# Attention with transposed AV in column tiles, packed exps and softmax sums gathered and broadcast by DMA

## Chip, cores, metric

One core of one Trainium2 chip. The time is the device time of one execution in microseconds (us). Executions of one kernel differ here, so each is listed with its mean granted TensorE clock (1.0 is full speed).

## The reference

Two independent parts, whose results are joined along the last axis. Part B (a state-space convolution, "the SSM") is the same in both kernels and runs first. Part A is attention over four segments of 512 rows, 32 heads of 18 numbers, with a memory carried from segment to segment:

```python
q, k, v = x @ wq, x @ wk, x @ wv              # 2048 x 576 -> 32 heads x 4 segments x 512 x 18
g = sigmoid(beta)                             # one gate per head
for s in range(4):
    p = softmax(q_s @ k_s.T * 18**-0.5 + causal_mask)
    a_dot = p @ v_s
    a_mem = (phi(q_s) @ M) / (phi(q_s) @ z + 1e-6)    # phi(t) = t + 1 if t > 0 else exp(t)
    o_s = g * a_mem + (1 - g) * a_dot
    M, z = M + phi(k_s).T @ v_s, z + phi(k_s).sum()
return concat(o) @ wo
```

## The kernel before

Four heads form a head group; each head has its own 32 rows of the array (18 used). Key block `kt` (128 keys) is scored against the queries from `128*kt` on, so a head's four blocks have 512, 384, 256 and 128 columns. V has a 19th column of ones, which makes the softmax sums. The product of the exps with V, called AV below, has the queries on partitions; so dividing by the sums is a product along the row, but the output must be transposed again before it meets `wo`.

```python
def scores_exp(s, hg, T, PT):
    for kt in range(4):
        for pr in range(2):                       # two heads to a score buffer
            pss = ps_s.tile([P, 2, L], F32, tag="s")
            for u in range(2):
                h4 = 2 * pr + u
                rows = slice(32 * h4, 32 * h4 + DH)
                nc.tensor.matmul(pss[:, u, P * kt:L], lhsT=T.kT[rows, hg, P * kt:P * kt + P],
                                 rhs=T.qT[rows, hg, P * kt:L], ..., tile_position=(32 * h4, 0))
            nc.scalar.activation(out=PT[kt][:, 2 * pr:2 * pr + 2, :], in_=pss[:, :, P * kt:L], func=ACT.Exp, ...)
        # [cut: causal mask of the diagonal block on GpSimd]

def av_retrieve(s, hg, T, PT, Oall, NDall, Mz_bd):
    po = ps_o.tile([P, 4, 4, DH + 1], F32, tag="o")
    for qt in range(4):
        for h4 in range(4):
            for kt in range(qt + 1):              # 40 matmuls of 19 columns
                nc.tensor.matmul(po[:, qt, h4, :], lhsT=PT[kt][:, h4, P * (qt - kt):P * (qt - kt) + P],
                                 rhs=T.Vaug[:, kt, 4 * hg + h4, :], ...)
    nc.vector.tensor_copy(out=Oall[:, :, 4 * hg:4 * hg + 4, :], in_=po[:])
    # [cut: retrieval from the memory, 4 matmuls of 76 columns, copied by ACT]

for s in range(NSEG):
    for hg in range(8):
        # [cut: allocation of PT]
        scores_exp(s, hg, T, PT)
        proj_chunk(s + 1, hg, Tn)                 # q, k, v, phi(k) of the next segment; none in segment 3
        av_retrieve(s, hg, T, PT, Oall, NDall, Mz_bd)
    # [cut: reciprocals and gates for the whole segment on DVE and GpSimd]
    for qt in range(4):                           # 5 transposes, their copies, 10 matmuls of 288 columns
        ...
```

The softmax here doesn't subtract the row's maximum and nothing guards it: scores larger than these inputs give would overflow.

Of the kernel before, what the change touches and what calls it, by code (L numbers as in the profile page):

```python
# [9 lines left out]
ALU = mybir.AluOpType  # L10
ACT = mybir.ActivationFunctionType
F32 = dt.float32
# [6 lines left out]
H = 32  # L19
# [16 lines left out]
def part_b(ctx, tc, B_q, B_k, B_v, B_shift_k, B_ssm_k, B_ssm_D, out, GB=288, debug=None):  # L36
# [25 lines left out]
    if debug == 'consts':  # L62
        nc.sync.dma_start(out=ov[:, 0, :], in_=CS[:, 0:9, :].rearrange('p a b -> p (a b)'))
        nc.sync.dma_start(out=ov[:, 1, :], in_=SN[:, 0:9, :].rearrange('p a b -> p (a b)'))
        nc.sync.dma_start(out=ov[:, 2, :], in_=CST[:, 0:9, :].rearrange('p a b -> p (a b)'))
        nc.sync.dma_start(out=ov[:, 3, :], in_=SNT[:, 0:9, :].rearrange('p a b -> p (a b)'))
        nc.sync.dma_start(out=ov[:, 4, 0:256], in_=W1bd[:].rearrange('p a b -> p (a b)'))
        nc.sync.dma_start(out=ov[:, 4, 256:320], in_=Psibd[:].rearrange('p a b -> p (a b)'))
        nc.sync.dma_start(out=ov[:, 4, 320:448], in_=ident[:])
        nc.sync.dma_start(out=ov[:, 5, :], in_=NSN[:, 8:17, :].rearrange('p a b -> p (a b)'))  # L70
        return
# [248 lines left out]
def part_a(ctx, tc, A_x, A_wq, A_wk, A_wv, A_wo, A_beta, out):  # L320
    nc = tc.nc
    consts = ctx.enter_context(tc.tile_pool(name="a_consts", bufs=1))
    segp = ctx.enter_context(tc.tile_pool(name="a_seg", bufs=2))
    accp = ctx.enter_context(tc.tile_pool(name="a_acc", bufs=1))
    hgp = ctx.enter_context(tc.tile_pool(name="a_hg", bufs=2))
    smallp = ctx.enter_context(tc.tile_pool(name="a_small", bufs=2))
    ps_s = ctx.enter_context(tc.tile_pool(name="a_ps_s", bufs=2, space=PSUM))
    ps_o = ctx.enter_context(tc.tile_pool(name="a_ps_o", bufs=1, space=PSUM))
    ps_j = ctx.enter_context(tc.tile_pool(name="a_ps_j", bufs=2, space=PSUM))

    scale = 1.0 / math.sqrt(DH)

    def load_w(w_ap, tail_at_64, nm):
        wt = consts.tile([P, 5, WPAD], BF16, tag=nm, name=nm)
        nc.vector.memset(wt[:, :, D:WPAD], 0.0)
        nc.sync.dma_start(out=wt[:, 0:4, 0:D], in_=w_ap[0:512, :].rearrange("(t p) f -> p t f", p=P))
        if tail_at_64:
            nc.sync.dma_start(out=wt[64:128, 4, 0:D], in_=w_ap[512:576, :])
        else:
            nc.sync.dma_start(out=wt[0:64, 4, 0:D], in_=w_ap[512:576, :])  # L340
        return wt

    wk_sb = load_w(A_wk, True, "wk_sb")
    wv_sb = load_w(A_wv, True, "wv_sb")
    wo_sb = load_w(A_wo, False, "wo_sb")

    def pad_w(w_sb, nm):
        wp = consts.tile([P, 5, H * 32], BF16, tag=nm, name=nm)
        nc.gpsimd.memset(wp[:], 0.0)
        nc.gpsimd.tensor_copy(out=wp[:, 0:4, :].rearrange("p t (h c) -> p t h c", c=32)[:, :, :, 0:DH],  # L350
                              in_=w_sb[:, 0:4, 0:D].rearrange("p t (h d) -> p t h d", d=DH))
        nc.gpsimd.tensor_copy(out=wp[64:128, 4, :].rearrange("p (h c) -> p h c", c=32)[:, :, 0:DH],
                              in_=w_sb[64:128, 4, 0:D].rearrange("p (h d) -> p h d", d=DH))
        return wp

    with tc.tile_pool(name="a_wtmp", bufs=1) as wtmp:
        wq_sb = wtmp.tile([P, 5, WPAD], BF16, tag="wq_sb", name="wq_sb")
        nc.sync.dma_start(out=wq_sb[:, 0:4, 0:D], in_=A_wq[0:512, :].rearrange("(t p) f -> p t f", p=P))
        nc.sync.dma_start(out=wq_sb[64:128, 4, 0:D], in_=A_wq[512:576, :])
        wq_pad = pad_w(wq_sb, "wq_pad")  # L360
    wk_pad = pad_w(wk_sb, "wk_pad")

    xT_all = consts.tile([P, 5, S], BF16)
    for t in range(5):
        c0 = 128 * t if t < 4 else 448
        nc.sync.dma_start_transpose(out=xT_all[:, t, :], in_=A_x[0, :, c0:c0 + P])

    def load_xT(s):
        return xT_all[:, :, L * s:L * (s + 1)]

    def kparts(t):
        return (slice(0, P) if t < 4 else slice(64, P))

    ident = consts.tile([P, P], BF16)
    nc.gpsimd.memset(ident[:], 0.0)
    nc.gpsimd.affine_select(out=ident[:], in_=ident[:], compare_op=ALU.not_equal, fill=1.0, base=0,
                            pattern=[[-1, P]], channel_multiplier=1)

    beta_bf = consts.tile([P, H], BF16)
    nc.sync.dma_start(out=beta_bf[:], in_=A_beta.partition_broadcast(P))  # L380
    g_bc = consts.tile([P, H], F32)
    nc.scalar.activation(out=g_bc[:], in_=beta_bf[:], func=ACT.Exp, scale=-1.0)
    nc.vector.tensor_scalar(out=g_bc[:], in0=g_bc[:], scalar1=1.0, scalar2=None, op0=ALU.add)
    nc.vector.reciprocal(out=g_bc[:], in_=g_bc[:])
    omg_bc = consts.tile([P, H], F32)
    nc.vector.tensor_scalar(out=omg_bc[:], in0=g_bc[:], scalar1=-1.0, scalar2=1.0, op0=ALU.mult, op1=ALU.add)

    Mz_f = consts.tile([P, 8, 19], F32)
    nc.vector.memset(Mz_f[:], 0.0)
    Mz_bds = [consts.tile([P, 8, 4 * (DH + 1)], BF16, tag="Mz_bd%d" % i, name="Mz_bd%d" % i) for i in range(2)]  # L390
    for i in range(2):
        nc.vector.memset(Mz_bds[i][:], 0.0)
    phikp = ctx.enter_context(tc.tile_pool(name="a_phik", bufs=1))

    def head_cols(w_pad, t, hg):
        return w_pad[kparts(t), t, 128 * hg:128 * hg + 128]

    o_view = out[0].rearrange("(j p) c -> p j c", p=P)

    class SegT:  # L400
        pass

    def alloc_seg(s):
        T = SegT()
        T.qT = segp.tile([P, 8, L], BF16, tag="qT")
        T.phiQ = segp.tile([P, 8, L], BF16, tag="phiQ")
        T.kT = segp.tile([P, 8, L], BF16, tag="kT")
        T.phiK = phikp.tile([P, 4, H * 32], BF16, tag="phiK")
        T.Vaug = segp.tile([P, 4, H, DH + 1], BF16, tag="Vaug")
        T.xT = load_xT(s)  # L410
        nc.gpsimd.memset(T.Vaug[:, :, :, DH:DH + 1], 1.0)
        if s < NSEG - 1:
            nc.gpsimd.memset(T.phiK[:], 0.0)
        return T

    def proj_chunk(s, hg, T):
        tok0 = 0
        xT = T.xT
        pq = ps_j.tile([P, L], F32, tag="pj")
        for t in range(5):  # L420
            nc.tensor.matmul(pq[:], lhsT=head_cols(wq_pad, t, hg), rhs=xT[kparts(t), t, tok0:tok0 + L],  # L421
                             start=(t == 0), stop=(t == 4))
        nc.vector.tensor_copy(out=T.qT[:, hg, :], in_=pq[:])  # L423
        if s > 0:
            e_sb = smallp.tile([P, L], BF16, tag="e_sb")
            nc.scalar.activation(out=e_sb[:], in_=pq[:], func=ACT.Exp)  # L426
            nc.vector.tensor_scalar(out=e_sb[:], in0=e_sb[:], scalar1=1.0, scalar2=None, op0=ALU.min)
            nc.vector.scalar_tensor_tensor(out=T.phiQ[:, hg, :], in0=pq[:], scalar=0.0, in1=e_sb[:],
                                           op0=ALU.max, op1=ALU.add)
        pk = ps_j.tile([P, L], F32, tag="pj")  # L430
        for t in range(5):
            nc.tensor.matmul(pk[:], lhsT=head_cols(wk_pad, t, hg), rhs=xT[kparts(t), t, tok0:tok0 + L],  # L432
                             start=(t == 0), stop=(t == 4))
        nc.scalar.copy(out=T.kT[:, hg, :], in_=pk[:])  # L434
        tt, half = hg // 2, hg % 2
        t0 = tok0 + P * tt
        c0 = 288 * half
        pv = ps_j.tile([P, 288], F32, tag="pj")
        for t in range(5):
            nc.tensor.matmul(pv[:], lhsT=xT[kparts(t), t, t0:t0 + P], rhs=wv_sb[kparts(t), t, c0:c0 + 288],  # L440
                             start=(t == 0), stop=(t == 4))
        nc.vector.tensor_copy(out=T.Vaug[:, tt, 16 * half:16 * half + 16, 0:DH],  # L442
                              in_=pv[:].rearrange("p (h d) -> p h d", d=DH))
        if s < NSEG - 1:
            pkt = ps_j.tile([P, 288], F32, tag="pj")
            for t in range(5):
                nc.tensor.matmul(pkt[:], lhsT=xT[kparts(t), t, t0:t0 + P], rhs=wk_sb[kparts(t), t, c0:c0 + 288],  # L447
                                 start=(t == 0), stop=(t == 4))
# [155 lines left out]
```

## Time and profile before

| | us | TensorE busy | ACT busy | DVE busy | mean clock |
|---|---|---|---|---|---|
| timed (three) | 620.52 median (619.65 to 628.27) | | | | |
| profiled execution | 637.5 | 82% | 48% | 47% | 0.728 |

A stage table of the profiled execution, from its windows. The columns are the window, its length, busy us (and instructions) of TensorE, its weight loads, DVE, ACT and GpSimd, then the clock, the DMA share and GB/s:

```profile
205.00:231.00 26.00, 5.54 (x13) 1.52 (x14) 1.92 (x8) 1.06 (x1) 18.97 (x11) 0.50 0.93 223
278.00:342.00 64.00, 58.80 (x561) 26.83 (x559) 30.80 (x62) 47.42 (x82) 20.91 (x31) 0.90 0.01 1
342.00:378.00 36.00, 36.00 (x265) 16.08 (x262) 13.49 (x51) 19.13 (x37) 9.12 (x10) 0.50 0.05 18
546.00:610.00 64.00, 52.40 (x509) 24.07 (x509) 11.08 (x28) 41.64 (x74) 24.39 (x32) 0.50 0.03 11
610.00:637.50 27.50, 15.91 (x60) 6.38 (x60) 9.85 (x21) 3.72 (x12) 0.00 (x0) 0.50 0.06 22
```

The start (205 to 231) is loading, with TensorE nearly idle. At a clock of 0.90 (second line) TensorE leaves 5 us of 64 idle; at half clock it is busy in all of 36 us (third). Segment 3 (fourth) and the last output product (fifth) are at half clock throughout.

### The profile page before, as it was taken

Reading aid. Unit: us, or ns where it says so; the run is one execution under the profiler, and the core shown is the slowest. Engines: PE = TensorE matmul, PEld = TensorE weight load, DVE = VectorE, ACT = ScalarE, POOL = GpSimd, SP = SyncE. Lnnn points to the kernel's source line nnn. Section 1 sums busy time; section 2 is a strip of 40 time slices with the busy share of each in tenths; the row PEclk is TensorE's granted clock in tenths of the full one; section 3 lists DMA queues with packets and bytes.
Section 4 is the critical chain, followed back from the end, with each engine's and each line's share of the span. In section 5 each row is a group of like instructions: output and inputs, shape, how many; then the busy total and the mean of one; then the engine's idle time right before and its main releaser. Section 6 shows DMA issues by size and latency. Waiting matters only on the chain.

```text
span 637.5 us, 9628 instructions
## 1 busy us (share of the span) xinstructions
PE 520.5 (82%) x3882; PEld 245.5 (39%) x3882; DVE 296.8 (47%) x611; ACT 302.9 (48%) x503; POOL 164.0 (26%) x189
## 2 busy tenths in 40 slices
PE   4186879799795179999997999999799999797646
PEld 1034547534474023434443443333344333343222
DVE  7994693734935023464444275332526433421041
ACT  2433523524233014437886545375645576647721
POOL 4000070000711900032333134121413222416310
PEclk9597999956998559959996558665556885555555
DMA  7978030040000930000000000000000000000000
GB/s 140 213 243 205 18 73 2 21 130 0 1 1 7 281 77 2 1 1 2 1 1 1 29 11 1 0 1 2 1 29 11 1 1 1 10 20 10 2 9 30
DMA packets 50431, 25.31 MB, mean 40 GB/s; under 512 B 32657, under 2 KB 49810, under 8 KB 50386
## 3 DMA queue, kind: packets, MB, share of 16 engines
q1 hardware_dynamic: 50386, 24.69, 15.9%
q8 instruction: 30, 0.49, 0.3%
q14 instruction: 15, 0.12, 0.1%
HBM read 9.75 MB, written 7.08 MB: 26 GB/s over the span
## 4 chain that ended last, share of the span: by engine, by line
PE 62%; DVE 16%; ACT 8%; issue 7%; POOL 3%; DMA 2%; SPq 2%; POOLq 0%; DVEq 0%; ACTq 0%
PE pss L464 10%; PE pout L556 7%; PE pk L432 6%; PE pq L421 6%; PE po L477 6%; ACT PT L466 5%; PE pv L440 5%; PE pkt L447 4%; DVE Y L269 2%; DVE A_sb L219 2%; PE ptr L545 2%; POOL PT L468 2%; DVE tmp L32 2%; PE pp L248 2%; PE ps L232 2%
## 5 line engine op out<-in xcount | busy, mean ns | idle before, releaser
L466 ACT ACTIVATE PT<-pss 128x1024 bf16<-128x1024 f32 (+3 forms) x256 | 171.9, 708 | 56.6 <-PE pss L464 55.1
L468 POOL TENSOR_SCALAR_AFFINE_SELECT PT<-PT 128x512 bf16<-128x512 bf16 x128 | 88.5, 695 | 260.6 <-ACT PT L466 250.1
L464 PE MATMUL pss<-qT,kT 18*128 18x256 bf16 (+3 forms) x512 | 99.6, 385 | 11.4 <-ACT PT L466 9.6
L421 PE MATMUL pq<-xT_all,wq_pad 128*128 128x512 bf16 (+1 forms) x160 | 59.0, 477 | 20.5 <-DMA xT_all<-in_A_x_dram 20.5
L477 PE MATMUL po<-Vaug,PT 128*128 128x19 bf16 x1280 | 52.6, 178 | 12.1 <-POOL PT L468 12.0
L276 POOL TENSOR_TENSOR Y<-xi_sb,H_sb 128x576 bf16<-128x576 bf16 x22 | 27.6, 1275 | 132.7 <-ACT xi_sb L275 132.2
L432 PE MATMUL pk<-xT_all,wk_pad 128*128 128x512 bf16 (+1 forms) x160 | 57.6, 453 | 1.4 <-DVE phiK L452 1.4
L477 PEld LDWEIGHTS <-PT 128*128 128x128 bf16 x1280 | 43.6, 103 | 33.6 <-POOL PT L468 23.2
L464 PEld LDWEIGHTS <-kT 18*128 18x128 bf16 x512 | 26.3, 96 | 63.0 <-issue 53.3
L556 PE MATMUL pout<-wo_sb,oT 128*128 128x288 bf16 (+1 forms) x160 | 46.9, 435 | 1.2 <-DVE oT L547 0.9
L423 DVE CAST qT<-pq 128x512 bf16<-128x512 f32 x32 | 22.1, 691 | 54.7 <-PE pq L421 30.5
L192 PE MATMUL ps<-kT,dg 128*128 128x512 bf16 x80 | 21.9, 438 | 23.4 <-DVE kvT L194 15.0
L440 PE MATMUL pv<-wv_sb,xT_all 128*128 128x288 bf16 (+1 forms) x160 | 34.0, 332 | 2.5 <-ACT kT L434 2.0
L479 DVE COPY Oall<-po 128x304 f32<-128x304 f32 x32 | 15.2, 474 | 43.3 <-PE po L477 43.0
L442 DVE CAST Vaug<-pv 128x288 bf16<-128x288 f32 x32 | 14.7, 460 | 43.3 <-PE pv L440 43.2
L421 PEld LDWEIGHTS <-wq_pad 128*128 128x128 bf16 (+1 forms) x160 | 14.6, 108 | 47.9 <-issue 26.1
L243 PE MATMUL pp<-A_sb,CS 128*128 128x288 bf16 x68 | 22.1, 326 | 13.1 <-ACT xi_sb L275 4.7
L232 PE MATMUL ps<-W1bd,xs 128*128 128x256 bf16 x144 | 23.2, 303 | 9.6 <-DMA xs<-in_B_ssm_k_dram 5.4
L547 DVE COPY oT<-ptr 128x128 bf16<-128x128 bf16 (+1 forms) x48 | 10.7, 222 | 40.0 <-PE ptr L545 40.0
L556 PEld LDWEIGHTS <-oT 128*128 128x128 bf16 (+1 forms) x160 | 17.8, 125 | 28.6 <-issue 21.4
L217 ACT CAST A_sb<-ps 128x1024 bf16<-128x1024 f32 x18 | 18.1, 1013 | 20.4 <-PE ps L232 20.1
L426 ACT ACTIVATE e_sb<-pq 128x512 bf16<-128x512 f32 x24 | 14.3, 596 | 28.1 <-DVE qT L423 28.1
(153 smaller groups left out, 787.3 us busy)
## 6 DMA issues: line engine op xcount, KB each, us to landing
q_sb<-in_B_q_dram SPq DMA_DIRECT2D x2, 1152.0 KB, 9.5
out_dram<-o_sb SPq DMA_DIRECT2D x2, 1152.0 KB, 7.2
out_dram<-outA SPq DMA_DIRECT2D x16, 144.0 KB, 1.7
kv_scratch<-kvT SPq DMA_DIRECT2D x4, 512.0 KB, 4.4
wq_sb<-in_A_wq_dram SPq DMA_DIRECT2D x1, 576.0 KB, 7.9
wk_sb<-in_A_wk_dram SPq DMA_DIRECT2D x1, 576.0 KB, 4.6
wv_sb<-in_A_wv_dram SPq DMA_DIRECT2D x1, 576.0 KB, 5.8
wo_sb<-in_A_wo_dram SPq DMA_DIRECT2D x1, 576.0 KB, 6.6
```

Of the source, the lines that this page charges most:

```text
L232: nc.tensor.matmul(ps[:, u, :], lhsT=xs[:, cc + u, :], rhs=W1bd[:].rearrange("p e k -> p (e k)"), start=True, stop=True)
L243: nc.tensor.matmul(pr, lhsT=CS[:, k1, :], rhs=A_sb[:, k1, :], start=True, stop=not (has_i or for_h))
L276: nc.gpsimd.tensor_tensor(out=Y4[:, k1, 2:4, :], in0=xi_sb[:].unsqueeze(1).to_broadcast([P, 2, GB]), in1=H_sb[:, k1, :, :], op=ALU.mult)
L421: nc.tensor.matmul(pq[:], lhsT=head_cols(wq_pad, t, hg), rhs=xT[kparts(t), t, tok0:tok0 + L], start=(t == 0), stop=(t == 4))
L432: nc.tensor.matmul(pk[:], lhsT=head_cols(wk_pad, t, hg), rhs=xT[kparts(t), t, tok0:tok0 + L], start=(t == 0), stop=(t == 4))
L440: nc.tensor.matmul(pv[:], lhsT=xT[kparts(t), t, t0:t0 + P], rhs=wv_sb[kparts(t), t, c0:c0 + 288], start=(t == 0), stop=(t == 4))
L447: nc.tensor.matmul(pkt[:], lhsT=xT[kparts(t), t, t0:t0 + P], rhs=wk_sb[kparts(t), t, c0:c0 + 288], start=(t == 0), stop=(t == 4))
L464: nc.tensor.matmul(pss[:, u, P * kt:L], lhsT=T.kT[rows, hg, P * kt:P * kt + P], rhs=T.qT[rows, hg, P * kt:L], start=True, stop=True, tile_ ...
L466: nc.scalar.activation(out=PT[kt][:, 2 * pr:2 * pr + 2, :], in_=pss[:, :, P * kt:L], func=ACT.Exp, scale=scale)
L468: nc.gpsimd.affine_select(out=PT[kt][:, :, 0:P], in_=PT[kt][:, :, 0:P], compare_op=ALU.is_ge, fill=0.0, base=0, pattern=[[0, 4], [1, P]], ...
L477: nc.tensor.matmul(po[:, qt, h4, :], lhsT=PT[kt][:, h4, P * (qt - kt):P * (qt - kt) + P], rhs=T.Vaug[:, kt, 4 * hg + h4, :], start=(kt == ...
L556: nc.tensor.matmul(pout[:], lhsT=oT[0:w, ft, :], rhs=wo_sb[0:w, ft, c0:c0 + 288], start=(ft == 0), stop=(ft == 4))
```

## The change

The intent: fewer and fuller instructions on the attention's path. The attention runs in sixteen slots, each for two head groups (a pair). A slot has ten exps of 1024 columns, which fill the score buffer, instead of sixteen of four widths; AV is turned round, so that V is the stationary operand, four heads work in four column tiles and the result has the head's numbers on partitions, ready for `wo` without a transpose. The softmax sums are then a row, one for each head, and dividing by them needs them on every partition of the head: they are gathered by small DMAs into a compact tile, inverted and gated, stored to DRAM and broadcast back. `wo` is laid out in eight padded groups. More changes with it: x is loaded by segment, the projections run two slots ahead and AV one slot behind, k is copied out by DVE instead of ACT, and four accumulation buffers serve projections, AV and output, where the kernel before had two for the projections and one each for AV and retrieval. Cut to its core:

```diff
-        for kt in range(4):
-            for pr in range(2):
-                ... nc.scalar.activation(out=PT[kt][...], in_=pss[:, :, P * kt:L], func=ACT.Exp)
+            for jj in range(2):                      # per head group: blocks 1 and 3 share a buffer
+                ps = self.ps_s.tile([P, 2, L], F32, tag="s", name="s1")
+                for b in range(2):
+                    mm(ps, b, 0, 2 * jj + b, u, 1)
+                for b in range(2):
+                    mm(ps, b, 384, 2 * jj + b, u, 3)
+                ex(p1[:, 2 * jj:2 * jj + 2, :], ps)
+        # block 2 of both head groups shares one (not shown)
-    nc.tensor.matmul(po[:, qt, h4, :], lhsT=PT[kt][:, h4, ...], rhs=T.Vaug[:, kt, 4 * hg + h4, :], ...)
+            for kt in range(4):
+                for j in range(4):
+                    nc.tensor.matmul(po[32 * j:32 * j + 32, P * kt:L], lhsT=V[:, kt, 19 * h:19 * h + 32], rhs=rhs,
+                                     start=(kt == 0), stop=(kt == 3), tile_position=(0, 32 * j))
+            nc.vector.tensor_copy(out=ou[:, u, 0, :], in_=po[:])
+        for j in range(4):                           # gather: 8 transfers
+            for u in range(2):
+                nc.sync.dma_start(out=cs[32 * j:32 * j + 16 * nk, u, :], in_=ou[32 * j + DH:..., u, :, :]...)
+        # [cut: reciprocal, times gate]
+        for j in range(4):                           # store: 8 transfers
+            for u in range(2):
+                nc.sync.dma_start(out=rd[j, u, 0:nk, :]..., in_=rb16[32 * j:32 * j + 16 * nk, u, :])
+        for j in range(4):                           # broadcast: 4 transfers
+            nc.sync.dma_start(out=rb[32 * j:32 * j + 32, :, :, :], in_=rd[j, :, 0:nk, :].partition_broadcast(32))
+        nc.vector.tensor_tensor(out=ou[:], in0=ou[:], in1=rb[:], op=ALU.mult)
-    nc.tensor.transpose(out=ptr[0:w, :], in_=o_seg[:, qt, P * ft:P * ft + w], identity=ident[:])   # and its copies
+    # beta is needed by partition: eight strided loads of 2-byte elements
+        for j in range(4):
+            nc.sync.dma_start(out=bt[32 * j:32 * j + 32, :], in_=gv[j].partition_broadcast(32))
+    def slot(self, i):
+        self.scores(s, p); self.proj_qk(i + 2); self.av(i - 1)
+        # then phi(k), memory update, v of the next segment, output product of the last one
```

## The prediction

> **What bounds the kernel now.** I read the span and the granted clock, then the page's slices, then the chain that ended last, then the groups by shape, then timelines of one head group. The page first:
>
> ```profile
> PE 520.5 (82%) x3882; PEld 245.5 (39%) x3882; DVE 296.8 (47%) x611; ACT 302.9 (48%) x503; POOL 164.0 (26%) x189
> PE   4186879799795179999997999999799999797646
> PEclk9597999956998559959996558665556885555555
> PE 62%; DVE 16%; ACT 8%; issue 7%; POOL 3%; DMA 2%; SPq 2%; POOLq 0%; DVEq 0%; ACTq 0%
> ```
>
> TensorE carries 62% of the chain and is nearly always busy from slice 15 on; that is the attention (the SSM ends near 205 us, and the change leaves it alone). The third line says that in most of the attention TensorE has a reduced clock. Reading windows of 4 us shows only two values, 1.0 and 0.5. Three longer windows:
>
> ```profile
> 230.00:610.00 380.00, 349.37 (x2755) 147.34 (x2754) 149.67 (x371) 225.98 (x398) 108.90 (x135) 0.68 0.02 6
> 306.00:337.00 31.00, 29.76 (x314) 14.38 (x312) 14.07 (x31) 26.58 (x46) 10.84 (x17) 1.00 0.00 1
> 426.00:446.00 20.00, 20.00 (x134) 6.88 (x132) 5.54 (x11) 11.66 (x19) 4.46 (x7) 0.50 0.00 1
> ```
>
> So the bound is TensorE throughout, with ACT close behind at full clock (26.6 of 31 us) and far behind at half (11.7 of 20). At full clock one head group takes 7.5 us (the pv groups in the chain start at 303.77 and 311.31), at half 11.6 us (431.65 and 443.27).
>
> The chain and the timeline give pitches, which the rows of groups do not: their means (385 ns, 477 ns) are latencies of overlapping matmuls.
>
> ```profile
> 303.77 0.82 PE pv L440 x5
> 308.25 0.54 PE pk L432 x2
> 303.13 0.32 PE po L477 x13
> 234.00 2.36 PE pq L421 x5
> 458.34 2.90 PE pout L556 x10
> L466 ACT ACTIVATE PT<-pss 128x1024 bf16<-128x1024 f32 x64 | 65.3, 1028 | 28.4 <-PE pss L464 28.3
> ```
>
> A 288-column matmul takes 164 ns at full clock and 285 at half; a 512-column one about 260 and 472. The 19-column AV matmuls take about 30 ns at either clock. The two row-tiled score matmuls of a pair overlap: a 512, 384, 256 or 128 pair takes 0.32, 0.27, 0.21, 0.16 us at full clock, and about 0.54, 0.43, 0.33, 0.22 at half.
>
> **What the Trainium skill says.** "TensorE: Matmul & The Clock Gate", Part 1, says that the clock has two states, half and full, chosen by activity in windows of about 3.4 us. The trace agrees on two states; but it also dropped to half at 420.6 and 519.8 us with no idle gap, so mere occupancy does not hold it up. Part 3 of that page gives 2.38x for three column tiles of 512 columns, and 3.07x for four row tiles; this trace has row pairs only (about 1.6x), no column tiles. "ScalarE: Activation LUTs", What ACT_TABLE_LOAD costs, gives 186 ns + 0.833 ns per column, and about 93 ns of overlap back to back. Agrees: 1028, 812, 602, 391 ns for 1024 to 256 columns. "DMA: Bandwidth & Descriptors", Anatomy of one DMA, has about 2 us of fixed cost; here a 1 KB load landed after 1.8 us, and five of them took SP 2.26 us to issue.
>
> **The change part by part.** I count for a slot, that is a pair of head groups, 16 in all.
>
> *AV.* Before, 80 matmuls of 19 columns, 80 x 30 ns = 2.4 us. After, 32 of 512/384/256/128 columns, in fours. One after the other at full clock they take 8 x (0.26+0.21+0.15+0.10) = 5.8 us; divided by 3.1 (an estimate that takes the skill's figure for four row tiles) 1.85 us, at half clock 3.3. At best 0.5 us is saved, and at half clock nothing.
>
> *Normalisation and output.* 80 transposes go (15+5 us busy) with their copies and the four-step waits on them. The output product contracts eight padded groups and not five, so 256 matmuls of 288 and not 160: 96 x 164 ns = +16 us, at half +27. The memory update becomes 384 tiny matmuls for 96, about 35 ns each, +8 us; but its 96 little DVE adds (16.4 us) become three.
>
> *Exps.* The same 163,840 columns in 160 instructions for 256: 96 x about 80 ns of pitch = 8 us of ACT. The k copies (19 us), retrieval copies (10) and half the output copies leave ACT, whose load falls from some 240 to 190 us.
>
> *DVE.* k copies (+22), k-for-phi copies (+10), AV and retrieval evictions of 512 columns (56 x 0.65 = 36 for 15), products with the broadcast sums (about 25): some 200 us for 160. Per slot about 13 us, below TensorE.
>
> *DMA.* 20 small transfers per slot, some 320. At 0.45 us of SP each, 9 us per slot. The chain gather (8), reciprocals, store (8), broadcast (4) is about 4+2+1+4+2+2+2 = 17 us. In the order of instructions the final product stands a slot later, behind the next pair's AV evictions, so I take it as hidden, except after the last pair.
>
> *TensorE's slot at full clock.* q and k 20 x 0.26 = 5.2; v 10 x 0.164 = 1.6; scores 3.84; AV 1.85: 12.5 us. In the order, the ten score groups are interleaved with 17 projection matmuls (8.3 us of TensorE) while ACT needs 10 x 0.93 + 1.0 = 10.3 us, so that phase is ACT's; AV, v and the rest follow with ACT idle, less two buffers of lead. I take 13.0. Phi(k) adds 1.6 and the memory update 1.1: **15.8 us in segment 0**. Retrieval 0.5 and output 16 x 0.164 = 2.6: **18.9 us in segments 1 and 2**. In segment 3: 14.5, 14.5, 13, 13.
> *At half clock* (TensorE alone binds): 9.4+2.85+6.1+3.3 = 21.7; with phi(k) and update 25.7; with retrieval and output 31.3; segment 3: 24.4, 24.4, 15, 15.
>
> *Start and tail.* Before, dense matmuls begin at about 231 us because five transposed loads of all of x must land. After, only 512 rows of x are loaded first, but wq's padding still waits for the SSM's memory: first matmul about 217. The prologue is 20 + 20 projection matmuls, 17 us (half: 30). The tail is 17 us of DMA chain, then 64 matmuls of 288 at half clock, 18 us, and 1 us: 36 us, for 28 before.
>
> Sum at full clock: 217+19+63+151+55+36 = **541 us** of profiled span. At half: 217+30+103+250+79+36 = **715**. Between them: with 60% of the time at full clock (mean 0.8), slots of 18.7, 22.5, 17.3 and 13.7 us give 217+20+75+180+62+36 = **590**; at mean 0.9, 561; at the old 0.68, 628. The timed runs were 620.5/637.5 = 0.973 of the profiled span. So 526 (full), 546 (0.9), 574 (0.8), 611 (0.68).
>
> I choose a mean clock near 0.84. The reason is density: in the stretch before that kept full clock, 4.2 of each 7.5 us were wide dense matmuls (56%); now it is about 13 of 18.9 us (q, k, v, phi(k), output, AV; 70%), and they come in one stretch of over 6 us each slot. Also the stops at the segment boundaries (334 to 342, 446 to 454, 542 to 550, where TensorE had 1.3 to 2.9 of 4 us) go. That gives **565 us**, 9% faster.
>
> **The rivals.**
> (a) *The clock stays as it is.* TensorE's own work hardly falls (AV and transposes give what output and update take), so if activity does not lift the clock the result is 611: within 2%. For it: at 522 to 610 us it never came back; score matmuls use 18 of 128 rows, and in the new score phase dense matmuls fill only about 45% at full clock. Against: the dense blocks. One chance in six.
> (b) *The column tiles do not overlap.* Weights of all four tiles use all 128 rows; if a load must wait for the matmul before it, AV is 5.8 us and not 1.85, 16 x 4 = 63 us more, so about 625. For it: no column tile in this trace. Against: the skill's measurement. One in ten.
> (c) *The DMA round trip shows.* If a small transfer takes 3 us rather than 2, or only a few are in flight, the chain exceeds 19 us, the strictly ordered DVE stands before the product or the reciprocal, and evictions and then TensorE wait: 2 to 4 us per slot, 30 to 60 us, so about 610. At most eight are outstanding in the order's waits. One in seven in full measure.
> (d) *Everything at full clock*, ACT and TensorE in balance: 526. One in eight.
>
> **Range and chances.** The middle of the sum is 565; (d) sets the low end at 520, (a) and (c) the high end at 612. Faster by over 2% (below 608) 0.85, within 2% 0.11, slower 0.04: slower needs (b) or (c) together with (a).
>
> **What would show it.** The SSM must end at the same time. Dense matmuls should begin at about 217 rather than 231. Mean clock between the start and the tail should be 0.8 to 0.9; if it is 0.68 and the slots are still short, my counts are wrong. Four po matmuls of 512 columns should take about 0.33 us at full clock together; 0.9 or more proves (b). Slots in segments 1 and 2 should be 19 to 25 us. ACT should be busy about 190 us in the attention, DVE 200. Waits of DVE on the gathered sums or the broadcast should be under 15 us in all but the tail; more proves (c). The tail after the last retrieval should be some 36 us, 8 longer than before. The prediction is wrong if AV or DMA is on the path in every slot, or if the clock does not follow density.

## More of the kernel before

The rounds of experiments ran on different chips, with the kernel before beside each; the changed kernel itself was timed in the first round only, so what is said against its 568 us goes across rounds. The best executions of the kernel before agree over all rounds within 2.1 us (618.9 to 621.0).

## The result

| | before | after |
|---|---|---|
| all executions, us | 620.52, 628.27, 619.65, 625.08 | 568.13, 577.36, 570.09, 567.85 |
| median | 622.8 | 569.11 |
| ratio of fast executions | | 0.9108 (0.9017 to 0.9199) |
| profiled execution | 637.5, slow, clock 0.728 | 566.4, fast, clock 0.840 |

Ratios here are the mean time of one kernel's fast executions over that of the other's in the same rounds, so not quite the ratio of the medians. The changed kernel is correct. Lines of its page, in the order of those that the prediction shows: busy times, TensorE's slices, the clock, the chain by engine, and the row of the exps.

```profile
PE 431.6 (76%) x3329; PEld 202.9 (36%) x3346; DVE 338.4 (60%) x631; ACT 246.6 (44%) x304; POOL 145.1 (26%) x179
PE   3085877968978735499979979989989999786215
PEclk9677999995599965669988976999969999967557
PE 41%; DVE 24%; DMA 12%; SPq 11%; issue 6%; ACT 5%; DVEq 0%; POOL 0%; ACTq 0%; POOLq 0%
L501 ACT ACTIVATE PT<-s 128x1024 bf16<-128x1024 f32 x160 | 150.7, 1048 | 87.3 <-PE s L497 83.0
```

The SSM ends near 205 us, as before. From slice 19 to slice 35 the clock is mostly 0.9, where before it was mostly 0.5 or 0.6. But TensorE is sparse in slices 15 to 17 and 37 to 40, and SP's queue and DMA together hold 23% of the chain, before 4%. The windows of start, attention and tail:

```profile
205.00:248.00 43.00, 20.80 (x62) 6.71 (x65) 7.90 (x21) 2.72 (x4) 23.85 (x12) 0.54 0.48 105
248.00:516.00 268.00, 240.80 (x2097) 94.24 (x2111) 176.54 (x366) 170.74 (x207) 85.09 (x124) 0.91 0.15 34
516.00:566.00 50.00, 19.94 (x114) 11.28 (x113) 18.16 (x34) 0.00 (x0) 0.00 (x0) 0.59 0.20 53
```

**The start** became longer, 43 us for 26. The chain of waits has this piece there (start, us, what):

```profile
220.89 17.37 DMA beta<-in_A_beta_dram
```

DVE's timeline shows what stood behind it. The brackets give DVE's idle time before the instruction and what ended it:

```profile
230.85 0.77 DVE L402 TENSOR_SCALAR gcol<-gcol 128x8 f32<-128x8 f32 x1 [6.78 <-ACT gcol L401]
...
238.60 0.17 DVE L402 TENSOR_SCALAR gcol<-gcol 128x8 f32<-128x8 f32 x1 [6.18 <-ACT gcol L401]
...
239.13 0.68 DVE L441 CAST k<-pk 128x512 bf16<-128x512 f32 x1
```

The first matmul did start at 215.4 us, but the copies of q and k stand on DVE, in order, behind the gate computation, and that behind the loads of `beta`: eight transfers of 0.5 KB in 2-byte elements, 10.5 us median from issue to landing. TensorE ran out of buffers and stood until the copies came; it works without a long stop from 239.9 us on, so 8 us of this window are projections already.

**The tail** became longer too: the last exp ends near 515 us and the kernel at 566. Part of its chain; "SPq" is SP's time for issuing one transfer:

```profile
494.17 0.42 SPq L585
495.61 0.37 SPq L588
496.08 2.94 DMA rb<-a_r_scratch
499.14 1.71 DVE ou L593
...
511.88 2.66 DMA rb<-a_r_scratch
514.66 1.24 DVE ou L593
...
525.33 2.92 DMA rb<-a_r_scratch
528.27 1.24 DVE ou L593
```

The products with the broadcast sums of the last five pairs start 11 to 16 us apart (499.1, 514.7, 528.3, 543.0, 553.9 us): not one transfer chain is exposed at the end, but several in series, each with eight stores of 0.46 us on SP one after the other, four broadcasts, and 2.7 to 2.9 us of landing.

DVE's waits on these transfers from 248 to 476 us (total us, times, longest):

```profile
DVE rc L577 <- DMA cs<-ou: 10.9, 4, 7.0
DVE rc L573 <- DMA cs<-ou: 8.9, 3, 6.5
DVE ou L593 <- DMA rb<-a_r_scratch: 1.6, 1, 1.6
```

And from 476 us to the end:

```profile
DVE ou L593 <- DMA rb<-a_r_scratch: 36.5, 5, 9.5
```

Beside the attention the round trip costs DVE little; at the end it is the path.

**AV.** A pair's 32 column-tiled matmuls at full clock, from TensorE's timeline (start, us, engine, line, what, count):

```profile
311.00 1.27 PE L551 MATMUL po<-PT,V 128*32 128x512 bf16 x32
```

At half clock a pair took 2.33 us (at 297.3), and in segments 1 to 3 at full clock twice 0.73. The four column tiles do work side by side.

### The profile page after: what moved, and what is told of

Read it like the earlier page. It is cut to its first block, busy times and chain, and to the rows that moved or that the text cites. A ratio compares the mean times of both kernels' runs of the same rounds, so it can differ in the third digit from the quotient of the medians.

```text
span 566.4 us, 8717 instructions
## 1 busy us (share of the span) xinstructions
PE 431.6 (76%) x3329; PEld 202.9 (36%) x3346; DVE 338.4 (60%) x631; ACT 246.6 (44%) x304; POOL 145.1 (26%) x179
## 4 chain that ended last, share of the span: by engine, by line
PE 41%; DVE 24%; DMA 12%; SPq 11%; issue 6%; ACT 5%; DVEq 0%; POOL 0%; ACTq 0%; POOLq 0%
PE pk L439 6%; PE pq L428 5%; PE s L497 5%; DMA rb<-a_r_scratch 4%; SPq L585 4%; SPq L413 4%; PE pout L604 4%; DMA beta<-in_A_beta_dram 3%; DVE Y L259 3%; PE pv L449 3%; DVE A_sb L209 3%; ACT PT L501 2%; PE pkt L463 2%; DVE tmp L32 2%; PE ps L222 2%
## 5 line engine op out<-in xcount | busy, mean ns | idle before, releaser
L501 ACT ACTIVATE PT<-s 128x1024 bf16<-128x1024 f32 x160 | 150.7, 1048 | 87.3 <-PE s L497 83.0
L504 POOL TENSOR_SCALAR_AFFINE_SELECT PT<-PT 128x512 bf16<-128x512 bf16 (+1 forms) x112 | 80.1, 729 | 179.1 <-ACT PT L501 179.1
L604 PE MATMUL pout<-wo_sb,oT 128*128 128x288 bf16 x256 | 42.1, 329 | 35.5 <-DVE oT L594 18.8
L497 PE MATMUL s<-q,k 18*128 18x256 bf16 (+3 forms) x512 | 58.3, 317 | 11.1 <-ACT PT L501 11.1
L428 PE MATMUL pq<-xT,wq_pad 128*128 128x512 bf16 (+1 forms) x145 | 55.6, 436 | 12.8 <-POOL wq_pad L345 10.9
L439 PE MATMUL pk<-xT,wk_pad 128*128 128x512 bf16 (+1 forms) x159 | 52.6, 420 | 6.4 <-POOL wk_pad L345 3.5
L604 PEld LDWEIGHTS <-oT 128*128 128x128 bf16 x256 | 27.4, 111 | 49.8 <-DVE oT L594 20.8
L449 PE MATMUL pv<-wv_sb,xT 128*128 128x288 bf16 (+1 forms) x160 | 34.0, 337 | 9.0 <-DVE k L441 6.1
L430 DVE CAST q<-pq 128x512 bf16<-128x512 f32 x32 | 22.0, 688 | 25.1 <-PE pq L428 25.0
L551 PE MATMUL po<-PT,V 128*32 128x256 bf16 (+3 forms) x512 | 25.6, 323 | 0.3
```

The source lines that it names most:

```text
L428: nc.tensor.matmul(pq[:], lhsT=self.wq_pad[self.kp(t), t, c:c + P], rhs=xT[self.kp(t), t, :], start=(t == 0), stop=(t == 4))
L439: nc.tensor.matmul(pk[:], lhsT=self.wk_pad[self.kp(t), t, c:c + P], rhs=xT[self.kp(t), t, :], start=(t == 0), stop=(t == 4))
L449: nc.tensor.matmul(pv[:], lhsT=xT[self.kp(t), t, P * tt:P * tt + P], rhs=self.wv[self.kp(t), t, 288 * h:288 * h + 288], start=(t == 0), st ...
L497: nc.tensor.matmul(ps[:, b, off:off + n], lhsT=k[r, u, P * kt:P * kt + P], rhs=q[r, u, P * kt:L], start=True, stop=True, tile_position=(32 ...
L501: nc.scalar.activation(out=dst, in_=ps[:], func=ACT.Exp, scale=self.scale)
L504: nc.gpsimd.affine_select(out=ap, in_=ap, compare_op=ALU.is_ge, fill=0.0, base=0, pattern=pat + [[1, P]], channel_multiplier=-1)
```

## The experiments

All but the two marked so gave the reference's result. The kernel before was timed beside each; its best executions were 618.9 to 621.0 us at a clock of 0.766 to 0.769, many others 628 to 629 at 0.75.

**1. The old kernel with the new AV alone** (wrong: the eviction, the copy out of the accumulation buffer, writes the result as if it were untransposed).

```diff
-            for h4 in range(4):
-                for kt in range(qt + 1):
-                    nc.tensor.matmul(po[:, qt, h4, :], lhsT=PT[kt][...], rhs=T.Vaug[:, kt, 4 * hg + h4, :], ...)
+        for kt in range(4):
+            for h4 in range(4):
+                nc.tensor.matmul(po[32 * h4:32 * h4 + 32, P * kt:L], lhsT=Vf[:, kt, v0:v0 + 32], rhs=PT[kt][:, h4, :],
+                                 start=(kt == 0), stop=(kt == 3), tile_position=(0, 32 * h4))
```

> The kernel before with nothing changed but the AV product: transposed, four column tiles, 16 matmuls per head group in place of 40; its result is copied as before and is wrong on purpose. In the middle of the attention the two kernels spend nearly the same TensorE time if it is counted at full clock (before 379 us x 0.68 = 258, after 266 x 0.92 = 245), so the gain there is the clock. Theory A: the old AV (40 short matmuls, each with a full weight load) is the sparse part that lets the clock fall. Then the mean clock between 231 and 610 us goes from 0.68 to 0.8 or more and the time to 565-590 us. Theory B: the stops at the segment boundaries and the scattered order of work let it fall. Then the clock stays within 0.05 of 0.68 and the time only falls by the shorter AV, 5 to 17 us, to 605-618.

Measured: 637.01 us (631.79 to 653.16), ratio 1.026 (1.014 to 1.038). Neither number was met: it was slower. Its fast executions had clocks of 0.740 to 0.764, no better than the kernel before. So the narrow old AV was not what kept the clock down, and in the old order the turned AV gains nothing.

**2. The changed kernel with the old AV orientation** (wrong, 80 matmuls of 32 columns per pair).

```diff
-                    nc.tensor.matmul(po[32 * j:32 * j + 32, P * kt:L], lhsT=V[:, kt, 19 * h:19 * h + 32], rhs=rhs, ...)
+                    for kt in range(qt + 1):
+                        nc.tensor.matmul(po[:, P * qt + 32 * j:P * qt + 32 * j + 32],
+                                         lhsT=pt[:, P * (qt - kt):P * (qt - kt) + P], rhs=V[:, kt, 19 * h:19 * h + 32], ...)
```

> The changed kernel with the old orientation of AV alone (80 matmuls of 32 columns per pair, probabilities as weights; wrong result on purpose, all copies and transfers as they are). Theory A: the clock between 250 us and the end of the exps falls from 0.92 to 0.75 or less, time 610-640. Theory B: the clock stays above 0.87; AV takes 80 x 30 ns = 2.4 us per pair in place of 1.35, 16 x 1.05 = 17 us, time about 586.

Measured: 587.75 us (585.03 to 593.44), ratio 0.950; mean clock 0.837 in the profiled execution, where the changed kernel has 0.840. In the attention alone (from 250 us to 2 or 3 us after the last exp) it had 286 us at 0.88 for 266 at 0.92. Theory A's 0.75 is out. The orientation is worth some 18 us; by time x clock about half of it is TensorE's own work, and the other half may be clock.

**3. Beta loaded once**, as 32 contiguous numbers to all partitions, the gates taken from it by partition.

```diff
-        for j in range(4):
-            nc.sync.dma_start(out=bt[32 * j:32 * j + 32, :], in_=gv[j].partition_broadcast(32))
+            nc.sync.dma_start(out=self.ball[:], in_=A_beta.partition_broadcast(P))
+        for j in range(4):
+            nc.scalar.activation(out=g[32 * j:32 * j + 32, :], in_=bv[32 * j:32 * j + 32, j, :], func=ACT.Exp, scale=1.0)
```

> The changed kernel with beta loaded once by one transfer of whole rows to all partitions and picked apart on ACT, in place of eight transfers of two-byte elements. If those transfers (17 us on the chain, VectorE standing behind them at 231 and 239 us) hold up the first eviction of k and v, steady work begins at about 230 and not 248 us, and the time falls by 12 to 18 us, to about 554. Rival: the weight loads, the padding and the memsets on GpSimd end at about 231 us anyway and take their place; then it falls by under 5 us.

Measured: fast executions 553.76 and 556.04 us, slow ones 566.77 and 569.91. Against the changed kernel's fast ones (567.85 to 570.09), 14 us: the start's added stop. In its profile (a slow execution: its SSM ended at 214 us, not 205) TensorE's last stop of over 2 us ended 6 us after its first projection matmul (at 230.4 us), where the changed kernel's ended 24 us after it (at 239.9).

**4. Nine small transfers per pair instead of twenty**, twelve in segment 0 (a layout of 64 columns that gathers, stores and broadcasts two head groups at once).

```diff
-            for u in range(2):
-                nc.sync.dma_start(out=cs[32 * j:32 * j + 16 * nk, u, :], in_=ou[32 * j + DH:..., u, :, :]...)
+            nc.sync.dma_start(out=cs[32 * j:32 * j + nr, :], in_=ou[32 * j + DH:32 * j + DH + 1, :, :, :]...)
-        # 8 stores
+            nc.sync.dma_start(out=rd.rearrange("j (c n) -> (j c) n", n=64), in_=rb16[:])
```

> The changed kernel with 9 transfers per pair for the softmax sums in place of 20 (4 gathers of 32 x 64 values, 1 store, 4 broadcasts), right result. If the chain of transfers, two thirds of it issue time of SP, sets the pace of the last five pairs (a product every 14 us from 499 to 555 us), each chain falls from 14 to about 9.5 us and the tail by 15 to 22 us, time about 550; the middle stays, as the chain is hidden there. Rival: the two buffers of the evicted AV and VectorE's order set that pace, and the tail falls by under 8 us.

Measured: 552.15 us (547.25 to 558.97), ratio 0.892. The tail of its profile:

```profile
510.00:545.00 35.00, 16.80 (x112) 9.77 (x109) 14.26 (x26) 0.53 (x1) 1.14 (x2) 0.72 0.23 69
```

It is 35 us instead of 50; counted from the last exp to the end, 35 instead of 53, of the 21 us by which the span fell. So nearly all of the gain lies at the end, where the chains stood in series.

**5. Wide dense work added to the kernel before.** Each q and k projection is computed twice into the same place, the second overwriting the first.

```diff
-        for t in range(5):
+        for t in list(range(5)) * 2:
             nc.tensor.matmul(pq[:], lhsT=head_cols(wq_pad, t, hg), ..., start=(t == 0), stop=(t == 4))   # and pk
```

> The kernel before with every q and k projection computed twice into the same place (the second pass overwrites the first, so the result is right): 640 more 512-column matmuls of 0.26 us at full clock, so wide dense matmuls are some 67% of a head group's TensorE time at full clock rather than 56%. Density theory (the reason the prediction gave for a better clock): the mean granted clock in the attention rises from 0.68 to over 0.8, and the time is only 650 to 670 us for 166 us of added full-clock work, of which 20 us go before the steady part. Rival (the clock does not follow density): it stays at 0.65 to 0.72, and 84 to 130 us in the steady part alone at that clock makes 740 to 790 us.

The count in that expectation is mine and wrong: the edit adds 320 matmuls, not 640, so 83 us at full clock and not 166 (TensorE's records of weight loads rise from 3882 to 4202). With the right count, and the attention of a fast execution (experiment 6: 361 us at 0.75, 271 at full clock), the density theory's clock of over 0.8 means (271 + 83)/0.8 = 442 us or less for the attention, so under 701 us in all; an unchanged 0.75 means 619 + 83/0.75 = 730. These two thresholds were worked out after the run. Measured: 698.76 us (695.96 to 708.18); clock from 231 to 670 us 0.81. The projecting part (to the first exp of segment 3), segment 3 and the output product in the windows of this kernel:

```profile
231.00:596.40 365.40, 345.27 (x2511) 142.02 (x2536) 134.64 (x337) 180.28 (x314) 76.89 (x101) 0.87 0.01 4
596.40:668.00 71.60, 54.80 (x536) 25.63 (x535) 17.67 (x36) 47.24 (x85) 31.62 (x34) 0.51 0.03 9
668.00:694.00 26.00, 15.92 (x60) 6.39 (x60) 8.66 (x19) 3.71 (x12) 0.00 (x0) 0.50 0.07 24
```

The same three stages of experiment 6, which stands for a fast execution of the kernel before:

```profile
231.00:521.70 290.70, 272.17 (x2189) 119.45 (x2211) 133.06 (x338) 177.25 (x317) 82.09 (x102) 0.80 0.02 5
521.70:592.00 70.30, 55.68 (x546) 25.59 (x544) 16.45 (x33) 46.78 (x82) 27.19 (x33) 0.52 0.03 10
592.00:619.00 27.00, 15.92 (x60) 6.39 (x60) 9.72 (x21) 3.73 (x12) 0.00 (x0) 0.50 0.06 22
```

Where dense work was added the clock rose from 0.80 to 0.87; where none was, it stayed at 0.50 to 0.52. TensorE's busy share hardly changed (0.94 and 0.94). In that part 83 us of full-clock work cost 75 us of time, where the old clock would have made 104. So dense work does raise the mean clock; but 75 us are what it would cost if it ran at full clock itself and the rest gained only some 8 us.

**6. The kernel before with score matmuls over 32 rows instead of 18** (the added rows are zeros).

```diff
-                    rows = slice(32 * h4, 32 * h4 + DH)
+                    rows = slice(32 * h4, 32 * h4 + 32)
```

> The kernel before with score matmuls over 32 rows of the array rather than 18 (the added 14 are zeros on both sides, so the result is right and the columns, so the TensorE time, are the same). Row theory (the clock follows the number of rows at work): the clock between 231 and 610 us rises from 0.68 to over 0.75, and the time falls under 605 us. Rival (rows that hold zeros, or rows at all, do not count): clock 0.66 to 0.70, time 615 to 630 us.

Measured: 619.76 us (618.1 to 621.09), clocks 0.766 to 0.775. The ratio is 0.985 (0.983 to 0.987) because six of the eight executions of the kernel before in those rounds were at 628 us; its best ones are 618.9 to 621.0 us at 0.766 to 0.769, the same. So zero rows don't better the best executions; that all four of this kernel were at that level, and one of eight of the other, is not explained. Whether rows with data would act is open. The whole attention of this profile, 231 to 592 us, had 0.75, and I use it below as the fast profile that the kernel before lacks.

**7. The changed kernel with its exps unpacked**: per pair sixteen, four each of 1024, 768, 512 and 256 columns.

```diff
-                for b in range(2):
-                    mm(ps, b, 0, 2 * jj + b, u, 1)
-                for b in range(2):
-                    mm(ps, b, 384, 2 * jj + b, u, 3)
-                ex(p1[:, 2 * jj:2 * jj + 2, :], ps)
+            for kt in range(4):
+                n = L - P * kt
+                for jj in range(2):
+                    ps = self.ps_s.tile([P, 2, L], F32, tag="s", name="s0")
+                    for b in range(2):
+                        mm(ps, b, 0, 2 * jj + b, u, kt)
+                    exv(dst[kt, jj], ps[:, :, 0:n])
```

> The changed kernel with its exps no longer packed: sixteen of 1024, 768, 512 and 256 columns per pair rather than ten of 1024, the same columns in all. 96 more ACT instructions of about 80 ns of fixed pitch are 8 us. Theory A (the score phase of each slot is bound by ACT and its two PSUM buffers): 6 to 12 us slower than the changed kernel, 575 to 581. Rival (TensorE or DVE binds the slot and ACT has slack): within 3 us, 566 to 572.

Measured: 619.83 us (613.66 to 620.44): 51 us slower where theory A had 6 to 12, and nearly all of the change's gain is gone. The windows of its attention, as a whole (to 3 us after the last exp, as in the changed kernel's) and from 300 to 355 us:

```profile
248.00:571.50 323.50, 295.99 (x2133) 109.20 (x2150) 186.75 (x373) 186.70 (x303) 89.71 (x124) 0.80 0.12 29
...
300.00:355.00 55.00, 54.56 (x253) 14.62 (x254) 27.23 (x55) 30.20 (x47) 13.40 (x18) 0.50 0.06 15
```

323.5 us at 0.80 are 258 us at full clock; the changed kernel's 268 at 0.91 are 244. At the changed kernel's clock 258 us would take some 282, so of the 55 us that the attention lost, some 14 are work and waits and some 41 are the clock. In the order of instructions the unpacked score blocks no longer fit beside the projections and spill between the AV and v matmuls of the same slot, which so lose their unbroken stretch. Whether the slower pace of the exps or this mingling matters is not separated, and experiment 2 speaks against the mingling as the whole cause: there the v and output stretches stand between narrow AV matmuls, and the clock was 0.88.

**8. The kernel before with its exps packed, and nothing else** (per head group four of 1024 columns and two of 512).

```diff
+        for i, kts in enumerate(((0,), (1, 3), (2,))):
+            n = sum(L - P * kt for kt in kts)
+            for pr in range(2):
+                # [cut: scores of the blocks kts, block 3 at column 384]
+                nc.scalar.activation(out=PT[i][:, 2 * pr:2 * pr + 2, :], in_=pss[:, :, 0:n], func=ACT.Exp, ...)
```

> The kernel before with its exps packed and nothing else: per head group four of 1024 columns and two of 512, instead of two each of 1024, 768, 512 and 256 (the two score blocks of 384 and 128 columns share a buffer); AV reads the same numbers. 64 ACT instructions fewer, 5 us of ACT, which is off the path wherever the clock is half. Clock theory (fewer, fuller score buffers and less ACT pacing pack TensorE's wide work closer, and this lifts the clock, as undoing the packing in the changed kernel cost 50 us by the clock alone): mean clock in the attention from 0.68 to over 0.78, time 560 to 595. Rival (packing matters only with the changed kernel's order and its slots of two head groups): clock 0.66 to 0.73, time 605 to 628.

Measured: fast executions 624.74 to 629.64 us at 0.741 to 0.745, ratio 1.012 (0.995 to 1.030). Near the rival's numbers; its clock of the attention is known from a slow execution alone (0.64 from 231 to 610 us). Packing by itself does nothing for the old order.

**9. The changed kernel with the k copies on ACT**, where the kernel before had them.

```diff
-            nc.vector.tensor_copy(out=k[:, u, :], in_=pk[:])
+            nc.scalar.copy(out=k[:, u, :], in_=pk[:])
```

> The changed kernel with the k projections copied out by ACT rather than DVE (32 copies of about 0.6 us; the kernel before had them on ACT). DVE theory (DVE, busy 4.4 to 4.9 of each 5 us in the first three segments, sets the slot): 556 to 564 us. ACT theory (the ten exps and their two buffers set the score phase, and what slows it thins out TensorE's work and costs clock, as the unpacked exps did): 1.2 us per slot are 19 us at least, and with the clock 585 to 610 us, mean clock in the attention under 0.88.

Measured: fast executions 570.96 and 575.25 us, slow ones 583.49 and 587.12, ratio 0.925 (0.910 to 0.940); clock in the attention 0.90. Both theories missed: DVE doesn't set the slot, and some 19 us more of ACT cost 4 (means of the fast executions) to 9 us (the ratios; their intervals overlap). So ACT's load as such isn't what took 51 us in experiment 7.

**10. Four output buffers instead of two.**

```diff
-        self.oup = pool("a_ou", 2)
+        self.oup = pool("a_ou", 4)
```

> The changed kernel with four output buffers rather than two, and nothing else. Of the 42 us that the combined version gained, beta (14) and transfers (17 to 20) explain 31 to 34. Buffer theory (the next pairs' evictions wait for a buffer that the transfer chain holds): 556 to 564 us. Rival (the rest of the gain is clock, won when the other two stops go together): 566 to 572 us.

Measured: fast executions 565.64 and 567.02 us, ratio 0.914: no effect. The rival.

**11. Experiments 3, 4 and 10 together.**

> The changed kernel with beta loaded once, nine small transfers per pair rather than twenty, and four output buffers rather than two. The parts alone took 13 to 14 us (beta) and 17 to 20 us (transfers). Theory A, that they lie at different ends of the kernel (the start and the tail) and add: 533 to 541 us, the buffers giving 0 to 5. Theory B, that both shorten the same wait or that the buffers bring the next stop: 545 to 552.

Measured: 527.3 us (524.41 to 531.03), ratio 0.839, clocks 0.868 to 0.889. This is below theory A's range and beats both kernels. The parts alone give 31 to 34 us and the whole 42; its attention had a clock of 0.95 for 0.91. Why it rose is not isolated; experiment 10 excludes the buffers alone.

**12. That version with two more stops removed**: beta loaded first and the gates computed after the prologue; the last output product starts with the six head groups that are ready.

```diff
+        self.ball = consts.tile([P, H], BF16, tag="ball", name="ball")   # before load_x and the weights
         a.prologue()
+        a.setup_g(tc, A_beta)
-        for qt in range(4):
-            self.out_proj(3, qt)
+        for lo, hi in ((0, 6), (6, 8)):           # 8 accumulators, head groups 0 to 5 first
+            ...
```

> The combined version (527.3 us) with two more stops taken away. Start: beta is loaded before x and the weights, and the gates are computed after the prologue, so that the copies of q and k no longer stand on DVE behind a wait for beta (about 5 us). Tail: the last segment's output product accumulates the six head groups that are ready while the last pair's transfer chain runs, and only 16 of 64 matmuls are left after it (48 x 0.164 = 7.9 us). Theory (both stops end on the path): 513 to 518 us. Rival (the next wait, for the padded weights at the start and the chain itself at the end, takes their place): 522 to 528 us.

Measured: 533.48 us (527.17 to 540.8), ratio 0.846. No gain. From its chain:

```profile
224.26 4.69 DMA wk_sb<-in_A_wk_dram
...
229.08 2.12 POOL wk_pad L345
...
519.01 6.67 PE pout L667 x32
```

At the start the load of `wk` and its padding took the place of beta, as the rival had it. At the end 32 matmuls, not 16, were left after the last product. The profiled executions of this and of experiment 11 also differ in the untouched SSM, in the window of 60 to 80 us. First experiment 11:

```profile
60.00:80.00 20.00, 18.10 (x119) 9.86 (x119) 11.99 (x13) 9.80 (x13) 0.00 (x0) 1.00 0.30 60
```

Then experiment 12:

```profile
60.00:80.00 20.00, 20.00 (x73) 7.34 (x70) 5.30 (x7) 4.50 (x8) 0.00 (x0) 0.50 0.24 50
```

The same instructions run at full clock in one execution and at half in the other, and the SSM ends 9.4 us later (215.3 us for 205.8). That is chance between executions; taken off, the spans are 522.7 and 522.3 us. The SSM also ended at 214 us in the profiles of experiments 1, 3 and 10, all slow. The clusters of the kernel before, 619, 628 and 637 us, lie 9 us apart and their mean clocks fall with them (0.77, 0.75, 0.74). But the SSM doesn't explain all of them: the profile of 637.5 us ended it at 205, and its 18 us more than experiment 6's lie in the attention (379 us for 361).

**When the clock switches.** In six profiles (the changed kernel and experiments 5 to 8 and 11) I took the clock of each microsecond of the attention, and from TensorE's timelines the share of time of wide dense matmuls (q, k, v, phi(k), output) in the 3.4 us that end 1 us before the first step at the new clock:

| switch | times | median share before it | |
|---|---|---|---|
| full to half | 26 | 0.30 | 24 of 26 at 0.54 or below |
| half to full | 24 | about 0.8 | 19 of 24 at 0.55 or above |

Wide dense means 288 or 512 columns over 64 or 128 rows. Experiment 8's profile was a slow execution. By the trace's own clock records, with the 3.4 us ended 0 to 1 us before the switch, the medians are 0.23 to 0.38 before a fall and 0.86 to 0.96 before a rise. TensorE's busy share, whatever it worked on, separates the switches as well: in the 3.4 us up to the switch it was 0.90 or less before 25 of 26 falls (median 0.63, never below 0.20) and 0.91 or more before every rise. So the table can't tell density from occupancy at a fall. Two things can: at half clock TensorE stayed busy for long without a rise (experiment 7), and in the first profile the clock fell at 519.7 us after 3.4 us with no idle time (the prediction's other case, at 420.6, did have 0.13 us of it).

The half-clock spells of the changed kernel lasted 7, 17, 10 and 10 us; two ended after 3.4 us of nothing but wide dense matmuls, the other two after a share of 0.41 and 0.55. The long ones of experiment 6 lasted 41, 48 and, to the end of the attention, 67 us. This is a correlation; experiment 5 is the intervention behind it.

As an average over the attention, density does not order the clocks. Recorded wide dense matmuls, at 0.26 and 0.164 us each, over time x clock:

| kernel | share | clock |
|---|---|---|
| experiment 6, for the kernel before | 0.52 | 0.75 |
| experiment 7, unpacked | 0.56 | 0.80 |
| the changed kernel | 0.58 | 0.91 |
| experiment 2, old AV in it | 0.58 | 0.88 |
| experiment 5, dense work added | 0.63 | 0.81 |

The same share goes with clocks from 0.80 to 0.91. What in the order of instructions makes the difference is open.

## Why the prediction was right or wrong

The total was right, 565 for 569.1, and so was the main effect (the clock rises). But its reason for the rise does not hold as it was counted, and the basis, the attention, the start and the tail were each off and cancelled: that the total came so close was luck. I use experiment 6's profile (619.4 us) as the fast kernel before.

- *The basis.* The profile was a slow execution, so the old clock of 0.68 in the attention was 0.75 in a fast one, and the factor 0.973 from profiled span to time was only that slow execution: after the change 568.13 us were timed for a span of 566.4. Without the factor my sum meant a span of 565/0.973 = 581 us, 15 too many.
- *The attention* was predicted between 269 us (full clock) and 317 (mean 0.8). It took 268 us at 0.91, which is 244 at full clock, so the work was overestimated by 9%. AV is one such term: 1.27 to 1.46 us per pair for an estimate of 1.85, and 5.8 one after the other. Another is a slip: the prologue of 17 us stands in the sum as 19. From the first exps of the slots, those of segments 1 and 2 took 18.5 us on average (314.3 to 462.5), below the 19 to 25 forecast. Rival (b) is dead.
- *The clock* was predicted to rise from density to about 0.84; it rose to 0.91 in the attention and 0.840 over the kernel. Against the fast kernel before the attention is 361 - 268 = 93 us shorter. At full clock the work fell from 361 x 0.75 = 271 to 244 us. At the old clock that work would have taken 244/0.75 = 325 us, so some 36 us come from less work and some 57 from the clock. Of the 36, some 19 are only moved, into the windows of the start (60 projection matmuls for 9) and the tail (16 output matmuls and a pair's AV and retrieval): an estimate from the matmuls recorded there. Rival (a) is dead. The step that failed is the count behind "density": 70% for 56% counts AV as dense after the change; without it the prediction's own numbers give 11.0 of 18.9 us, 58%, and the traces 0.58 for 0.52. That added dense work raises the mean clock is shown (experiment 5), and that this change's gain in clock needs packing and the new order together (experiments 7 and 8). Why they do is open: my finer reason, that the narrow old AV thinned the work out, fell with experiments 1 and 2, experiment 7 lost the clock at nearly the same share, and the single stretch in each slot, the other half of the reason, was not tested by itself. Nor were the stops at segment boundaries, the projections two slots ahead or the four accumulation buffers.
- *The start* failed: "dense matmuls should begin at about 217". One began at 215.4, but steady work only at 239.9, 9 us later than in the kernel before (231); the window to 248 is 17 us longer. I took the weights' padding as the last wait and overlooked the eight loads of beta, and DVE's order behind them; 14 us came back with one load (experiment 3).
- *The tail* failed: predicted 36 us with one chain of 17 us exposed, measured 42 from the last retrieval (524 us), the prediction's own mark, and 50 as windowed. The step that failed is "hidden, except after the last pair". The chains of the last five pairs ended 11 to 16 us apart, in series; nine transfers instead of twenty gave 17 to 20 us (experiment 4).
- *Rival (c)* was right about what costs and wrong about where: waits on the gathered sums and the broadcast were 10.9 + 8.9 + 1.6 us and 4.5 us for segment 0's products in the attention up to 476 us: 25.9 us, over the 15 that I had named as proof of (c). By that sign (c) came in part. The chain of waits from 248 to 476 us also gives the round trip 16% (landing 10%, SP's issue 6%). But it was worth little there: nine transfers instead of twenty brought the last exp only 2.8 us earlier (510.5 us for 513.3, experiment 4). At the end DVE waited 36.5 us.
- *The engines*: DVE 176.5 us in the attention and 18 in the tail for "200", ACT 170.7 for 190. DVE is not the bound (experiment 9).

Added up: start +17, attention -93, tail +23 is -53 us, the difference of the two spans (619.4 and 566.4).

## What to carry to other kernels

Before you work from a profile, see which state its execution was in: here its clock, and a conversion factor read from it, were those of a slow one. Count TensorE's work at full clock, apart from the clock; here a new order of instructions was worth more through the clock (57 us) than the work that it saved, and undoing one part of it (the packing) cost about as much as the whole change had gained (51 us), some 41 of it through the clock. Don't carry over more of the reason than the runs show: dense work added raised the clock, but the average share of dense work did not tell which order would get the better clock. A transfer chain that hides beside a busy stretch comes back, several times over, where the work runs out: look at the first and the last 50 us by themselves.

## What the Trainium skill lacked or had wrong

- "TensorE: Matmul & The Clock Gate", Part 1, lets the clock fall after an idle window. Here no fall came after an idle one: TensorE was busy in 20 to 97% of the 3.4 us before each of 26 falls, and in all of them at 519.7 us of the first profile; and the clock stayed at half with TensorE busy in 54.56 of 55 us (experiment 7). The page speaks of busy-ness; what it doesn't have is the share of wide dense matmuls, 0.30 before a fall and about 0.8 before a rise. It also gives the ramp little weight (under 1% of a kernel); here the clock that one 20 us stretch happened to get was 9 us, 1.5%.
- The same page, "A second HAM failure mode: psum-queue depth-cycling", has a clock that oscillates with micro-idles between groups. Experiment 7 is near to it (more, smaller score groups through the same two buffers, clock 0.80 for 0.91), but its long half-clock spell had hardly any idle time (0.44 of 55 us).
- The same page, Part 3, has three column tiles (2.38x) and four only together with four row tiles. Here 32 matmuls in four column tiles took 1.27 us, against 5.8 estimated one after the other: about 4.5x, more than four tiles can give, so the estimate is too high; but near four.
- "DMA: Bandwidth & Descriptors", Anatomy of one DMA, has about 2 us of fixed cost for transfers that GpSimd issues, and no sum for SP's, which all of these are. The small transfers here landed after 1.4 us (store), 1.8 (gather) and 2.7 (broadcast), but what made the chain long was SP's issue, 0.37 to 0.59 us for each. For loads in 2-byte elements I found no time on the page; those of beta took 10.5 us for 0.5 KB.
